# Another order for every engine of a scheduled attention-and-FFT kernel, and waits written latest first

## The chip, the cores and the metric

The kernel runs on one core of a Trainium2 chip. The metric is device time in microseconds (us) of one launch. Before the change three runs gave 243.01, 243.37 and 244.91 us; the median is 243.37. PE is TensorE's matmul stream, PEld its weight loads, DVE VectorE, ACT ScalarE, POOL GpSimd, and SP the SyncE queue, which issues nearly all DMAs.

## The reference

Two branches read the same x (2048 x 640, bf16) and are mixed by a gate per token.

```
g = sigmoid((x * gate_w).sum(-1))
# A: 32 heads of 20, four segments of 512 tokens
for s in range(4):
    p = softmax(q[s] @ k[s].T * scale + causal_mask);  a_dot = p @ v[s]
    a_mem = (phi(q[s]) @ M) / (phi(q[s]) @ z + 1e-6)      # phi(t) = t+1 if t>0 else exp(t)
    o = sigmoid(beta) * a_mem + (1 - sigmoid(beta)) * a_dot
    M += phi(k[s]).T @ v[s];  z += phi(k[s]).sum(0)
a = concat(o) @ wo
# B: a filter in the frequency domain
b = irfft2(rfft2(x) * (w_r + 1j * w_i))
return g * a + (1 - g) * b
```

## The kernel before

The kernel is a list of some 2,300 recorded operations. Each names the engines that may run it with a fixed and a per-element cost, what it reads and writes, and the PSUM banks that it holds. The tuple `ORDER` lists all operations in sequence; a number is twice the operation's index, plus one if it takes the second of its engines. So `ORDER` sets both the order on every engine and who does what. `Sched.schedule` walks the per-engine queues with a cost model, and from the modelled times it chooses PSUM banks (two pools of four, `qk` for scores and `gen` for everything else) and DMA semaphores. `Sched.emit` then writes the instructions, each with the waits that its producers on other engines and its predecessors in a bank or buffer require. Engines run their queues strictly in order.

By segment the operations are as follows.

- `project`: q and k by `proj` (five matmuls of 512 columns, contraction over xT; `projd` for the first two head groups), copied out by `ev_proj` (on ACT, line 523, or DVE, line 525), stored to DRAM (`st_qk`) and loaded back padded to head strips (`pad`, `pad2`). `phi_exp`, `phi_max` and `phi_min` make phi; phi(k) is transposed by DMA (`pkT`, tile `pkn`). `vproj` gives V, which DVE scales (`ev_v`, line 1115).
- `attend`: per pair of head groups five score units (`qk`), their exponentials on ACT (line 1263), causal masks on POOL (line 1284), and the product with V: `pvf` in segments 0 to 2, `pv` in segment 3. In segments 0 to 2 the unnormalised result is copied (`ev_pv`) and stored (`st_u`, tensor u_scr).
- `denominators` of segments 0 to 2: `ld_den` brings the row sums from u_scr, DVE inverts them (`den_rec`, line 1211) and applies the gate (`den_gate`, line 1213, tile `rc`), `st_r` stores `rc` to r_scr.
- `mem_read` (`memrd`) and `mem_update` (`mupd`, from `pkn` and V): the compressive memory.
- `fft`: folds of x on DVE or POOL (lines 901, 906), `F1`, `D`, `T`, the multiplication by the weights (line 1439), `Tb`, `Db` with the G sums (line 1485). Their copies are `ev_F1`, `ev_D`, `ev_Tb`, `ev_Db`.
- `finish_tile` for four token tiles of each segment: `ld_r` brings r_scr back as tile `r`, `ld_u` brings u_scr as `oU`, five `normal` multiply the two (line 1526), the memory part comes by a transposing DMA (`oT`, tile `mT`) and is added (`addmem`, line 1534), and `Fb` plus five `oproj` (lines 514 and 512) accumulate B and A in one bank; `final` copies it out and `st_out` stores it. Segment 3 goes on the chip (`oT3`, `ev_oT3`) with its own copy of wo (`ld_wo2`, 800 KB), and its tiles are stored by `st_part`.

Matmuls use three tile shapes (full array, 20-row strips of `qk`, 32-column strips); a change of shape has a cost in the model (`COST`). The launch begins with ten matmuls on zeros. In `emit` the waits of one operation were written in the order of how much each implies:

```
for key, (val, vc) in sorted(waits.items(), key=lambda q: -len(q[1][1])):
```

Of the kernel before, what the change touches and what calls it, by code (L numbers as in the profile page):

```python
# [12 lines left out]
P = 128  # L13
# [36 lines left out]
class Sched:  # L50
    HOP = 70.0
# [57 lines left out]
    COST = {(0, 1): 94.0, (0, 2): 94.0, (1, 0): 110.0, (1, 2): 110.0, (2, 0): 110.0, (2, 1): 94.0}  # L109

    def schedule(self, pools, order, nsem=56):
# [31 lines left out]
        port = mode = 0  # L143
        level = {k: {q: 0.0 for q in v} for k, v in pools.items()}
# [23 lines left out]
        def head(e):  # L168
# [4 lines left out]
            for p in o.preds:  # L173
                if p.t1 is None:
                    return None
                if p.eng != "pe" or e != "pe":
                    t = max(t, p.t1 + self.HOP)
# [9 lines left out]
            if o.dma:  # L187
                gate = window()
                if gate is not None:
                    t = max(t, gate.t1 + self.HOP)  # L190
            if e == "dve" and o.lock:
                t = max(t, free["pool"])
            elif e == "pool":
                t = max(t, port)
            return t

        while len(self.order) < len(order):
# [21 lines left out]
            if e == "dve" and o.lock:  # L219
                port = t + occ  # L220
            if o.dma:
# [4 lines left out]
                o.t1 = max(ring[:o.width])  # L226
# [11 lines left out]
            o.t1 += lat  # L238
            self.order.append(o)
            for b in o.banks:  # L240
                b.left -= 1
                if b.left == 0:
                    for q in range(b.bank, b.bank + b.n):
                        users[q] = list(b.ops)
                        level[b.pool][q] = max(p.t1 for p in b.ops) + self.HOP
# [3 lines left out]
    def emit(self, *last):  # L249
# [14 lines left out]
        for o in self.order:  # L264
# [3 lines left out]
            for p in o.preds + o.dyn:  # L268
# [5 lines left out]
                if waits.get(key, (0, None))[0] < val:  # L274
                    waits[key] = (val, vc)
            for key, (val, vc) in sorted(waits.items(), key=lambda q: -len(q[1][1])):
                if k.get(key, 0) >= val:
                    continue
                sem = dsem[key] if isinstance(key, int) else prog[key]
                self.eng[e].wait_ge(sem, val)  # L280
                for kk, vv in vc.items():
                    if k.get(kk, 0) < vv:
                        k[kk] = vv
                k[key] = val
            h = o.alts[e][0](self.eng[e])
# [176 lines left out]
class Kern:  # L462
# [34 lines left out]

    def mms(self, items, r, w, prio, name="", extra=0.0, mode=0):

        cost = sum(c * PECOL + 0.75 if mode > 0 else max(c * PECOL + 2.8, 25.4) for _, c in items) + extra  # L500
# [15 lines left out]
        op = self.Sc.op({"pe": (f, cost, 141.0)}, r=r, w=w, prio=prio, name=name, mode=mode)  # L516
        return op

    def copy_alts(self, dst, src, n, engines=("act", "dve"), scale=None):

        alts = {}
        if "act" in engines:
            alts["act"] = (lambda e: e.activation(dst(), src(), ACT.Copy), 65 + 0.833 * n, 110.0)
# [10 lines left out]
    def either(self, fn, n, r, w, prio, name="", after=()):  # L534

        return self.Sc.op({"dve": (fn, 67 + 0.52 * n, 68.0), "pool": (fn, 120 + 1.95 * n, 50.0)}, r=r, w=w, prio=prio, name=name, after=after, lock=True)
# [5 lines left out]
    def dma(self, dst, src, nbytes, r, w, prio, tr=False, name="", after=(), queue="sp"):  # L542
# [14 lines left out]
        "ld_fcat": (400.0, 350.0, 16), "ld_g": (400.0, 1500.0, 16), "ld_gc": (580.0, 200.0, 16), "ld_gw": (420.0, 600.0, 16),  # L557
        "ld_hm": (600.0, 850.0, 16), "ld_r": (570.0, 500.0, 16), "ld_tt": (530.0, 1650.0, 16), "ld_u": (500.0, 450.0, 16),
        "ld_wka": (520.0, 1100.0, 16), "ld_wkb": (450.0, 2200.0, 16), "ld_wqa": (500.0, 1100.0, 16), "ld_wqb": (500.0, 2200.0, 16),
        "ld_wo": (600.0, 700.0, 16), "ld_wo2": (600.0, 3000.0, 16), "ld_wv": (450.0, 3000.0, 16), "ld_x": (450.0, 950.0, 16),  # L560
        "oT": (1300.0, 750.0, 16), "pad2": (370.0, 350.0, 10), "pad": (400.0, 1250.0, 10), ("pkT", 131072): (1260.0, 600.0, 16), ("pkT", 262144): (1280.0, 1100.0, 16),
        ("st_qk", 65536): (450.0, 220.0, 16), ("st_qk", 131072): (480.0, 350.0, 16), ("st_qk", 262144): (480.0, 720.0, 16), "st_g": (430.0, 150.0, 4), "st_o": (660.0, 950.0, 8), "st_out": (560.0, 1900.0, 4),
        "st_part": (430.0, 250.0, 16), "st_r": (480.0, 200.0, 16), "st_u": (520.0, 700.0, 16), ("xT", 131072): (1240.0, 1300.0, 16), ("xT", 262144): (1700.0, 2300.0, 16),
# [16 lines left out]
        46, 0, 90, 26, 74, 23, 2, 4, 36, 24, 6, 8, 28, 10, 12, 72, 14, 16, 30, 18, 20, 178, 64, 34, 202, 66, 68, 44, 42, 70, 93, 214, 52, 190, 48, 94,  # L580
        204, 97, 216, 180, 192, 218, 104, 98, 182, 76, 206, 101, 194, 38, 208, 220, 196, 103, 198, 222, 201, 184, 224, 186, 210, 188, 296, 50, 212,
        256, 298, 362, 78, 300, 536, 32, 80, 274, 538, 258, 83, 302, 260, 262, 276, 130, 278, 264, 84, 54, 280, 106, 266, 282, 1904, 86, 304, 364,
        284, 88, 366, 108, 380, 306, 576, 132, 826, 268, 290, 828, 814, 110, 368, 578, 831, 816, 113, 382, 384, 386, 819, 370, 540, 388, 832, 270,
        834, 410, 412, 272, 836, 414, 416, 391, 418, 552, 372, 490, 420, 288, 492, 494, 114, 496, 498, 554, 118, 820, 822, 134, 336, 500, 240, 137,
        338, 242, 340, 120, 348, 58, 824, 342, 116, 350, 308, 122, 312, 544, 142, 226, 932, 546, 124, 344, 292, 244, 56, 228, 144, 246, 286, 248, 347,
        139, 352, 230, 294, 232, 126, 250, 354, 146, 234, 374, 1906, 149, 237, 1908, 356, 254, 1910, 359, 2094, 151, 238, 1912, 844, 1914, 252, 2124,
        140, 2126, 1916, 2128, 128, 2130, 360, 166, 2096, 40, 846, 2098, 154, 2132, 848, 2100, 2134, 1924, 326, 1926, 314, 2102, 168, 392, 1928, 2104,
        1930, 156, 892, 310, 1932, 152, 838, 1944, 1934, 170, 334, 1946, 158, 894, 840, 324, 316, 1948, 842, 808, 897, 161, 328, 810, 1950, 1952, 394,
        320, 813, 880, 886, 163, 882, 322, 1954, 888, 560, 332, 502, 884, 504, 396, 506, 330, 172, 508, 890, 448, 376, 510, 1936, 398, 450, 436, 512,
        438, 378, 402, 452, 514, 562, 440, 174, 442, 2162, 400, 1962, 2164, 176, 444, 2166, 516, 556, 454, 456, 2168, 446, 165, 2170, 458, 464, 460,  # L590
        466, 406, 1918, 468, 462, 470, 570, 472, 408, 2172, 910, 912, 542, 474, 898, 900, 318, 914, 602, 903, 2150, 548, 604, 2152, 2154, 2156, 2158,
        1920, 2178, 572, 404, 2160, 1966, 2180, 1958, 2182, 1922, 1968, 574, 904, 60, 2184, 2174, 2186, 906, 594, 2188, 1956, 564, 908, 1970, 2176,
        580, 934, 874, 596, 876, 1972, 879, 476, 566, 1974, 62, 478, 480, 550, 1977, 868, 870, 930, 422, 568, 482, 424, 873, 484, 426, 928, 916, 558,
        486, 428, 430, 488, 918, 2136, 432, 598, 2138, 920, 2140, 434, 2142, 856, 582, 858, 1960, 2144, 922, 519, 861, 924, 606, 584, 2146, 936, 1938,
        520, 2148, 926, 588, 523, 1020, 525, 608, 586, 652, 591, 2596, 802, 654, 862, 850, 804, 864, 852, 1940, 2216, 867, 2204, 2206, 2218, 2208,
        2220, 1942, 2210, 2222, 1980, 854, 2224, 2212, 656, 634, 2226, 2214, 1978, 778, 658, 2006, 2228, 636, 780, 2230, 2008, 1982, 2190, 2010, 782,
        2012, 526, 946, 2014, 786, 784, 2192, 948, 1964, 938, 940, 942, 2194, 788, 950, 2196, 945, 2198, 952, 600, 660, 2017, 2200, 790, 662, 2202,
        792, 2018, 976, 978, 1984, 794, 2020, 958, 798, 796, 1986, 960, 980, 954, 2233, 800, 1988, 982, 610, 956, 664, 2038, 612, 1990, 528, 2236,
        2234, 1992, 965, 530, 984, 986, 2040, 1995, 534, 2076, 988, 2078, 962, 2042, 1996, 2000, 1998, 2044, 991, 614, 618, 1016, 2080, 2024, 620,
        2002, 996, 1014, 2082, 2238, 638, 998, 2084, 972, 2004, 2022, 2046, 622, 668, 974, 992, 624, 2086, 2049, 2056, 626, 1018, 994, 1070, 1072,  # L600
        2058, 1074, 666, 2060, 1022, 1076, 642, 1002, 2050, 806, 1104, 1024, 1026, 670, 645, 1001, 2062, 532, 1028, 2270, 2064, 1031, 628, 2036, 2636,
        2252, 2240, 1106, 2272, 630, 2638, 2274, 2254, 640, 2066, 2276, 2106, 676, 616, 2640, 2256, 678, 592, 2258, 1010, 1004, 2243, 2026, 966, 968,
        2052, 2070, 2028, 1013, 632, 692, 971, 1006, 694, 680, 2244, 2642, 1009, 2644, 686, 1032, 2068, 1034, 682, 2246, 646, 1100, 2054, 2090, 1036,
        2030, 2088, 684, 2288, 649, 710, 2034, 2646, 672, 2290, 1039, 2566, 712, 674, 2292, 2598, 2294, 2600, 2306, 2072, 2602, 2110, 2604, 2308,
        2606, 2074, 2568, 2310, 700, 2092, 2108, 2312, 714, 2608, 726, 2112, 2786, 703, 716, 728, 2114, 1044, 2788, 2570, 688, 1062, 1064, 1046, 2790,
# [1001 lines left out]
```

## Time and profile before

| | before |
|---|---|
| median of 3 runs | 243.37 us |
| span of the profiled execution | 245.4 us |
| mean granted TensorE clock | 0.986 |
| instructions | 10243 |
| DVE, ACT, POOL busy | 195.6, 199.9, 166.4 us |
| DMA moved | 42.17 MB |

One execution was profiled; its own time is known only as its span, which is 2.0 us above the median and 0.5 us above the slowest of the three runs. A busy share is an average over stages. PE's busy time includes modelled ends of pipelined matmuls, so a gap of PEld (the weight loads, which run ahead) often shows a wait better than a gap of PE.

### The profile page before, as it was taken

Reading aid. Unit: us, or ns where it says so; the run is one execution under the profiler, and the core shown is the slowest. Engines: PE = TensorE matmul, PEld = TensorE weight load, DVE = VectorE, ACT = ScalarE, POOL = GpSimd, SP = SyncE. Lnnn points to the kernel's source line nnn. Section 1 sums busy time; section 2 is a strip of 40 time slices with the busy share of each in tenths; the row PEclk is TensorE's granted clock in tenths of the full one; section 3 lists DMA queues with packets and bytes.
Section 4 is the critical chain, followed back from the end, with each engine's and each line's share of the span. In section 5 each row is a group of like instructions: output and inputs, shape, how many; then the busy total and the mean of one; then the engine's idle time right before and its main releaser. Section 6 shows DMA issues by size and latency. Waiting matters only on the chain.

```text
span 245.4 us, 10243 instructions
## 1 busy us (share of the span) xinstructions
PE 228.8 (93%) x4347; PEld 140.8 (57%) x4361; DVE 195.6 (80%) x481; ACT 199.9 (81%) x241; POOL 166.4 (68%) x297
## 2 busy tenths in 40 slices
PE   7899999999999999999899999899999997699994
PEld 2574567765455665545556555465454565366794
DVE  0479998889999987989999898989889867435563
ACT  2289698988999999999899889999999976388740
POOL 8513268557969846768947998859898694359730
PEclk9999999999999999999999999999999999589999
DMA  7999959975799875575698661375758997812123
GB/s 168 278 365 208 239 160 178 318 140 164 210 200 174 168 226 143 125 199 135 202 233 234 185 186 53 99 210 146 222 151 194 230 140 96 127 36 85 57 84 108
DMA packets 58928, 42.17 MB, mean 172 GB/s; under 512 B 30020, under 2 KB 55172, under 8 KB 58884
## 3 DMA queue, kind: packets, MB, share of 16 engines
q1 hardware_dynamic: 57844, 40.96, 69.2%
q8 instruction: 34, 0.56, 1.0%
q10 hardware_dynamic: 1040, 0.57, 0.8%
q14 instruction: 10, 0.08, 0.1%
HBM read 23.32 MB, written 12.30 MB: 145 GB/s over the span
## 4 chain that ended last, share of the span: by engine, by line
PE 54%; DVE 18%; ACT 12%; DMA 10%; issue 3%; SPq 1%; DVEq 0%
PE psum L514 48%; ACT ex L1263 9%; PE psum L512 6%; DMA pkn<-phk 4%; DMA r_scr<-rc 3%; DMA xT<-in_A_x_dram 2%; DVE xsb L906 2%; DVE Pt L1439 2%; DVE xf L901 1%; DVE phk L1085 1%; ACT et L1072 1%; DVE oU L1526 1%; DVE G L1485 1%; DVE ub L525 1%; DVE va L1115 1%
## 5 line engine op out<-in xcount | busy, mean ns | idle before, releaser
L1263 ACT ACTIVATE ex<-psum 128x2048 bf16<-128x2048 f32 (+4 forms) x92 | 138.7, 1507 | 16.3 <-PE psum L514 14.3
L1284 POOL TENSOR_SCALAR_AFFINE_SELECT ex<-ex 128x256 bf16<-128x256 bf16 (+2 forms) x224 | 122.1, 567 | 42.0 <-ACT ex L1263 38.4
L514 PE MATMUL psum<-qkp 20*64 20x64 bf16 (+5 forms) x1280 | 32.7, 271 | 4.8 <-issue 2.3
L514 PE MATMUL psum<-xT,wk 128*128 128x256 bf16 (+1 forms) x280 | 34.0, 273 | 0.9 <-DMA wk<-in_A_wk_dram 0.6
L514 PE MATMUL psum<-wv,xT 128*32 128x321 bf16 (+3 forms) x400 | 30.0, 301 | 0.6 <-DVE va L1115 0.3
L514 PE MATMUL psum<-xT,wq 128*128 128x512 bf16 (+1 forms) x121 | 27.0, 380 | 1.3 <-DMA xT<-in_A_x_dram 0.7
L1439 DVE TENSOR_TENSOR Pt<-psum,Wt 128x642 bf16<-128x642 f32 x32 | 25.5, 820 | 2.3 <-PE psum L514 1.9
L514 PEld LDWEIGHTS psum<-qkp 20*64 20x64 bf16 x1280 | 13.4, 103 | 19.5 <-ACT ex L1263 13.2
L514 PEld LDWEIGHTS psum<-xT,wk 128*128 128x128 bf16 (+1 forms) x280 | 19.9, 97 | 7.0 <-DMA wk<-in_A_wk_dram 1.1
L512 PE MATMUL psum<-wo,oU 128*32 128x320 bf16 x480 | 23.4, 313 | 0.5 <-DVE oU L1534 0.5
L906 POOL TENSOR_TENSOR xsb<-xf 128x320 bf16<-128x320 bf16 (+2 forms) x12 | 9.2, 763 | 17.1 <-DVE xsb L906 13.2
L525 DVE CAST ot<-psum 128x320 bf16<-128x320 f32 x21 | 10.1, 491 | 12.9 <-PE psum L512 10.5
L514 PEld LDWEIGHTS psum<-wv,xT 128*32 128x32 bf16 (+1 forms) x400 | 14.3, 96 | 8.3 <-issue 2.4
L514 PE MATMUL psum<-big,Ac 128*128 128x160 bf16 (+2 forms) x96 | 18.1, 258 | 0.7 <-DVE Pt L1439 0.3
L1115 DVE TENSOR_TENSOR va<-psum,ebx 128x320 bf16<-128x320 f32 x32 | 15.2, 483 | 4.2 <-ACT gate L1113 2.1
L514 PE MATMUL psum<-big,Cp 128*128 128x321 bf16 (+1 forms) x96 | 18.0, 302 | 0.2 <-DVE G L1485 0.2
L514 PE MATMUL psum<-ex,va 128*32 128x64 bf16 (+3 forms) x576 | 17.4, 256 | 0.7 <-DVE dn L1152 0.3
L1485 DVE TENSOR_TENSOR G<-eo,psum 128x320 bf16<-128x320 f32 x32 | 14.7, 482 | 3.9 <-PE psum L514 2.8
L512 PEld LDWEIGHTS psum<-wo,oU 128*32 128x32 bf16 x480 | 12.4, 100 | 8.8 <-issue 4.2
L514 PE MATMUL psum<-tt,Yt 128*128 128x256 bf16 (+1 forms) x96 | 16.5, 275 | 0.3
L514 PEld LDWEIGHTS psum<-ex,va 128*32 128x32 bf16 x576 | 11.1, 96 | 9.7 <-POOL ex L1284 3.4
L1072 ACT ACTIVATE et<-qu 128x512 bf16<-128x512 bf16 x25 | 15.6, 630 | 0.2
(99 smaller groups left out, 391.9 us busy)
## 6 DMA issues: line engine op xcount, KB each, us to landing
qkp<-qk_scr SPq DMA_DIRECT2D x28, 160.0 KB
tt<-tab_tt SPq DMA_DIRECT2D x8, 512.0 KB, 4.3
qk_scr<-qu SPq DMA_DIRECT2D x12, 256.0 KB, 3.1
u_scr<-ub SPq DMA_DIRECT2D x12, 256.0 KB, 3.9
xsb<-in_A_x_dram SPq DMA_DIRECT2D x8, 320.0 KB, 6.8
oU<-u_scr SPq DMA_DIRECT2D x15, 128.0 KB, 2.9
out_dram<-ot SPq DMA_DIRECT2D x12, 160.0 KB
Wt<-in_B_w_r_dram SPq DMA_DIRECT2D x16, 80.2 KB, 2.6
```

The lines of the kernel that those rows point to most:

```text
L512: h = e.matmul(dst, wt, r_, start=st, stop=sp_, **{**kw, "tile_position": (0, q), "skip_group_check": True})
L514: h = e.matmul(o_, l_, r_, start=st, stop=sp_, **kw)
L525: alts["dve"] = (lambda e: e.tensor_copy(dst(), src()), 67 + 1.04 * n, 68.0)
L901: self.either(lambda e, r=r, op=op: e.tensor_tensor(xf.ap(r * 642, [321, 2], [1, 320]), xs.ap(o, [D, 2], [1, 320]), xs.ap(o + 320, [D, 2], ...
L906: self.either(lambda e, dst=dst, src=src, d0=d0, n=n, op=op: e.tensor_tensor(xs.ap(o + dst, [D, 2], [1, n]), xf.ap(src + d0, [321, 2], [1, ...
L1072: self.one("act", lambda e: e.activation(et.ap(0, [1, L]), qsl(), ACT.Exp), L, [qb], [b("et", pi_)], late, name="phi_exp")
L1085: fmin = lambda e: e.tensor_tensor(dst(), dst(), et.ap(0, [1, L]), ALU.min)
L1115: self.one("dve", lambda e: e.tensor_tensor(va.ap(i * H * VW + h0 * VW, [VW, nh], [1, DH]), self.ps(bank, 0, [DH, nh], [1, DH]), self.ebx. ...
L1263: self.one("act", lambda e, d=d, q=q: e.activation(self.ex.ap(*d), self.ps(bank, *q), ACT.Exp, scale=SC), n, [bank], [self.exb(s, 2 * pr + ...
L1284: self.one("pool", lambda e: e.affine_select(self.ex.ap(e0 + d0, [1280, 4], [1, n], np_=np_), self.ex.ap(e0 + s0, [1280, 4], [1, n], np_=np_),
L1439: self.one("dve", lambda e, ri=ri, Pt=Pt, Wt=Wt, wo_=wo_, bank=bank: e.tensor_tensor(Pt.ap(ri * 322, [644, 2], [1, KD]), self.ps(bank, 0, ...
L1485: self.one("dve", lambda e, q=q, n2=n2, bank=bank, eo=eo: e.tensor_tensor(self.G.ap(n2 * D + 639 * q, [1 - 2 * q, 320]), eo.ap(q, [1, 320] ...
```

## The change

No operation is added or taken away. Four things differ.

1. `ORDER` is another sequence. On PE 210 of the 1072 adjacent pairs of operations are kept, on DVE 45 of 480, on ACT 77 of 248, on POOL 55 of 292, on SP 17 of 231. The middle displacement is 5 operations or so on PE, 11 on DVE, 6 on ACT, 4 on POOL, 3 on SP. 14 more operations run on DVE, 11 fewer on ACT's queue (12 fewer copies, and the load of `wk` that was on SP), 2 fewer on POOL, 1 fewer on SP.
2. The model's constants are changed, which moves bank choices and DMA semaphores, since these follow the modelled times: a delay per pair of engines in place of one delay, landing of a DMA 500 ns later, DVE and POOL overlapping at the shared port by some ns, costs of a few operations.
3. The waits of one operation are written in the order of the modelled time at which they end, latest first.
4. The `m_mask` products on POOL (line 1361) are marked `lock` for the model.

The start of the orders, and the two stretches that the prediction speaks of:

```
SP before:  ld_x1 xT0 ld_beta ld_wka xT1 xT2 ld_wkb ld_x0 ld_fcat ld_x4 ld_x2 ld_wv ...
SP after:   xT0 xT1 xT2 ld_x1 ld_wkb ld_x0 ld_beta ld_x2 ld_wv ld_x3 ld_fcat ld_x4 ...
ACT before: ld_wqa exp(beta) ev_projd ...
ACT after:  ld_wqa ld_wka ev_projd ev_projd exp exp(beta) ...

SP before:  ld_den oT ld_u ld_wo2 st_g pad oT ld_u ld_u ld_u ld_u ld_u st_r st_out pad oT ld_r st_out st_out oT oT ld_g st_out oT oT
SP after:   ld_den ld_u ld_u pad ld_u ld_u ld_u ld_u st_r pad oT ld_r st_out ld_wo2 oT ld_g st_out st_out oT st_out oT st_out oT

DVE before: den_rec normal G G den_gate normal pv_den pv_rec normal pv_mul addmem addmem G ev_Db G final final G
            pv_den G pv_rec pv_mul final [5 normal] pv_den pv_rec pv_mul addmem ...
DVE after:  den_rec G normal normal normal den_gate G addmem G addmem G G pv_den pv_rec pv_mul ev_Db G G
            [5 normal] final pv_den pv_rec pv_mul addmem G G pv_den G pv_rec G pv_mul addmem ...
```

The diff, cut to its core:

```diff
 class Sched:
-    HOP = 70.0
+    HOPS = {
+        "pe": {"pe": 0.0, "act": 52.0, "dve": 55.0, "pool": 60.0, "sp": 60.0, "dma": 50.0},
...
+    FREE, PORT, LATE = 52.0, (85.0, 55.0), 500.0
...
-                    t = max(t, p.t1 + self.HOP)
+                    t = max(t, p.t1 + self.HOPS[e]["dma" if p.dma else p.eng])
...
-                o.t1 = max(ring[:o.width])
+                o.t1 = max(ring[:o.width]) + self.LATE
...
-            for key, (val, vc) in sorted(waits.items(), key=lambda q: -len(q[1][1])):
+            kept = []
+            for key, (val, vc, t1) in sorted(waits.items(), key=lambda q: -len(q[1][1])):
                 if k.get(key, 0) >= val:
                     continue
-                sem = dsem[key] if isinstance(key, int) else prog[key]
-                self.eng[e].wait_ge(sem, val)
+                kept.append((t1, dsem[key] if isinstance(key, int) else prog[key], val))
...
+            for t1, sem, val in sorted(kept, key=lambda q: -q[0]):
+                self.eng[e].wait_ge(sem, val)
...
     ORDER = (
-        46, 0, 90, 26, 74, 23, 2, 4, 36, 24, 6, 8, 28, 10, 12, 72, 14, 16, 30, 18, 20, 178, 64, 34, 202, 66, 68, 44, 42, 70, 93, 214, 52, 190, 48, 94,
...
+        4626, 4628, 4542, 4540, 4647, 4630, 4584, 4556, 4633, 4546, 4544, 4600, 4568, 4570, 4572, 4654, 4648, 4602, 4558, 4604, 4574, 4652, 4606,
```

## The prediction

> **What bounds the kernel now.** I read the page first: busy shares, the 40 slices, the chain. Then one table of stretches, the chain of waits in order of time, and the timeline of the SP queue late in the span.
>
> ```profile
> span 245.4 us, 10243 instructions
> ...
> PE 228.8 (93%) x4347; PEld 140.8 (57%) x4361; DVE 195.6 (80%) x481; ACT 199.9 (81%) x241; POOL 166.4 (68%) x297
> ...
> PE   7899999999999999999899999899999997699994
> ...
> PEclk9999999999999999999999999999999999589999
> ...
> PE 54%; DVE 18%; ACT 12%; DMA 10%; issue 3%; SPq 1%; DVEq 0%
> ```
>
> TensorE (PE) bounds it: 93% busy, and it carries over half of the chain. Its two bad slices (7 and 6) lie near 205 us, and right there the granted clock falls to 0.5 and 0.8. The stretches say how much is idle where (columns: stretch, its length, busy us and instructions of PE, PEld, DVE, ACT, POOL, granted clock, DMA share, GB/s):
>
> ```profile
> 0.00:12.00 12.00, 9.24 (x134) 4.65 (x135) 3.29 (x7) 2.64 (x5) 8.82 (x13) 1.00 0.89 220
> 24.00:204.00 180.00, 172.85 (x3081) 103.33 (x3093) 160.40 (x396) 164.64 (x197) 133.73 (x246) 1.00 0.74 181
> 204.00:216.00 12.00, 8.71 (x197) 5.16 (x200) 7.07 (x18) 5.68 (x9) 4.29 (x6) 0.73 0.80 105
> 216.00:240.00 24.00, 24.00 (x732) 18.19 (x728) 12.47 (x31) 16.14 (x20) 16.04 (x27) 0.99 0.22 66
> ```
>
> PE idles 2.76 us in the first 12 us, 7.15 us in the 180 us of the middle, 3.29 us in 204 to 216. In that last stretch some 4.8 us of work (211.4 to 216.2) also ran at clock 0.50. The chain of waits, in order of time (start, length, what), names the causes at both ends:
>
> ```profile
> 3.61 4.16 DMA xT<-in_A_x_dram
> ...
> 193.49 0.31 DVE rc L1213
> ...
> 194.85 6.89 DMA r_scr<-rc
> 201.74 0.02 issue
> 201.76 2.35 DMA r<-r_scr
> ...
> 209.06 2.35 issue
> ```
>
> At the start, PE works on the second transposed piece of x, issued only at 3.61. Late, the softmax denominators of segment 2 go out (`st_r`, from `rc`) and come back (`ld_r`): from the end of `rc` (193.80) to the first product with it (204.13) 10.3 us pass. The row "issue" is a stall of PE with no release behind it; one packet of PE's instruction queue was under way (208 to 210: one packet, 1.2 us). The timeline of the SP queue (start, length of the issue) shows what stood ahead of `st_r`:
>
> ```profile
> 187.79 0.60 SPq L548 DMA_DIRECT2D wo<-in_A_wo_dram  x1
> ...
> 189.25 2.33 SPq L546 DMA_TRANSPOSE mT<-o_scr  x1
> 191.63 3.17 SPq L548 DMA_DIRECT2D oU<-u_scr  x5
> 194.85 0.60 SPq L548 DMA_DIRECT2D r_scr<-rc  x1
> ```
>
> **The change part by part.** The matmuls are the same 4361, and in the two orders the changes between the three tile shapes number 229 and 230. At a change the weight load idles 0.20 to 0.27 us in the timeline, so this costs at most 0.3: nothing.
>
> *Who copies.* Twelve PSUM copies move from ACT to DVE on balance (six of `ev_D`, six of `ev_Tb`, three `ev_oT3`, one each of `ev_proj` and `ev_projd`, less one `ev_pv` and four `final`), and DVE gains four folds and a `normal`, and loses a gate table and two adds. By the rows (ACT 0.54, 0.60, 0.59; DVE 0.52, 0.68, 0.69; `final` 0.44 and 0.49) ACT loses about 7 us and DVE gains about 9: ACT 193, DVE 204 of 245. Neither passes PE's 229, so I cost it at nothing. The cover is DVE's remaining fifth; gone for one copy, it costs 0.7.
>
> *Start.* On SP the second and third transposes stood behind an `xsb` load (0.40), the first transpose (1.22), `beta` (0.57) and `wk` (0.42); now they stand behind the first transpose alone, and `wk` goes out on ACT's queue. The second can be issued at about 0.79+1.22 = 2.0 in place of 3.61: 1.6 us sooner. If the DMA engines (share 0.89 over 12 us) were the limit, nothing is won. I take 1.2, nearer the queue's end, because the `xsb` load that shared the engines now comes behind. `beta` moves later by some 4 us; its first user, the V copy at 20.3, hides it.
>
> *Waits.* The built program keeps the wait that is written first on the instruction itself and puts the others into a semaphore instruction ahead of it. PE has 80 instructions with two or more waits (now 81). In the trace such a semaphore instruction takes 51 ns on PE and the next weight load begins typically 25 ns later. With the latest first, 76 ns go wherever the other order stood and PE really waited: between 0 and 80 x 0.076 = 6.1. PE waits for POOL 13 times, the kind with a partner wait; half of those: 0.5.
>
> *Middle.* Of PE's adjacent pairs only 210 of 1072 stay, but attention keeps its place (counted by PE work done, most scores move under 1 us); fillers are permuted. The memory update of segment 1 moves 1 to 6 us later, behind its transposed load `pkn` (1.4 us of PE and PEld waits). What the rest does no row shows: not more gain than half of the idle 7.15, and as much loss if fresh waits of the present size (42 waits for ACT, 0.3 each) appear in a quarter more places. I take 1.0, from -3.5 to +3.5, near the `pkn` row.
>
> *End.* Before `st_r` SP issued, after `ld_den` (185.27): two transposes (1.29, 2.33), six `ld_u`, the 800 KB load of `wo2`, and two small ones, 9.6 us in all; `st_r` left 1.05 us after `rc` into engines with a share of 1.19 (192 to 198), and took 6.89. Now only six `ld_u` and one `pad` stand between, 4.4 us with gaps, while `rc` needs about 3.8 (landing of u_scr loads, median) + 3.4 (DVE work up to `rc`) = 7.2 after `ld_den`. SP then waits for `rc`, and the backlog has 2.8 us to drain. Landing: 1.8 (40 KB stores) to 6.9; I take 3.0, near the small stores, for `st_r` is 32 KB. With `ld_r` at 2.6 the 10.3 us become 5.7. In DVE's new order 5.2 us of work fill that time, then come the five `normal`, then `final`, `pv_den`, `pv_mul`, the G sums. So DVE idles 0.5, where before it idled 1.41, and PE's 0.5 us wait for the add at 208.09 goes. The stall of 2.35 and the half clock's cost (4.8 us of work at 0.5: 2.4) I count half: a fetch that comes late under DMA load can come late again, but with no wait ahead of it the hole is shorter. End: 0.5 + 2.4 = 2.9, between -5.5 and +8.
>
> The row: 0.9 us of PEld waiting, then 2.6, and the clock was 0.50 for the next windows. The Trainium skill (TensorE: Matmul & The Clock Gate, Part 1) says that the clock halves after an idle window of about 3.4 us; the trace agrees in size, with 3.3 us of waits nearly back to back. By that rule a hole of 2.35 alone would keep the clock and the end would give 4.1 instead.
>
> Sum: 1.2 + 0.5 + 1.0 + 2.9 = 5.6; the profiled span would be 239.8. The span lies 2.0 above the median (243.37) and 0.5 above the slowest run (244.91). If the timed runs hold the late hole, they go to 243.37 - 5.6 = 237.8; if none does, to 243.37 - 2.7 = 240.7. Their spread of 1.9 settles neither; I take the middle, 239.2.
>
> **The rivals.**
> *Only the start comes.* The middle gives nothing and the late hole stays or was never in the timed runs: 243.37 - 1.2 - 0.5 = 241.7, and up to 245 if the middle loses. For it: PE is 96% busy in the middle, and every fine interlock there is new; also if waits in another order change nothing. Against: the SP rows.
>
> *The denominators come late and now block DVE.* On the other side. The five `normal` stood behind `final`, `pv_mul` and two G sums, and now stand ahead of them. Those free the four general PSUM banks. If `st_r` again takes 6.9, the wait is 6.9 + 2.8 = 9.7 against 5.2 of work: DVE stops for 4.5 us, PE runs out of banks about 1 us later, idles 3.5, and the clock halves for 6.8 us (3.4 lost). Also `wo2` is now issued right behind `ld_r`, ahead of two mT transposes: 800 KB at about 200 GB/s are 4 us for a load that lands in 3.8 to 7.2. Price: 3.5 + 3.4 + 4 = 10.9, less the 5.3 of the old hole, less 1.7 of start and waits: +3.9 on a run with the old hole and more on one without: about 248. It decides when `r` lands over 3 us later than DVE's cover.
>
> *The middle closes too.* Half of its idle time goes (3.5 in place of 1.0), and the whole late hole: 235.5. For it: PE has no other bound above 204 us of DVE.
>
> **How the numbers follow.** Forecast 0.44, only the start 0.27, late denominators 0.17, middle too 0.12. One per cent (2.43 us) is about what a measurement tells from no change. Faster (under 240.94): nearly all of the forecast's cases and of the last: 0.54. Same: the start alone, and a little of the forecast: 0.29. Slower (over 245.8): 0.17. The range 235 to 246 takes in the first two cases and half of the last, and leaves out about 0.06 below and 0.14 above. The forecast's own range is 237 to 241.
>
> **What would show it.** Start right: the second transpose issued near 2.0 and PE's first dense stretch about a microsecond earlier. End right: `r_scr` lands in under 4 us, DVE's wait for `r` is under 1 us, no 0.5 in the clock row past slice 30. Waits right: fewer short PEld waits on semaphores of two engines. Wrong: DVE waiting 3 us or more for `r`, PE behind it on a bank, or a new half-clock stretch in the middle; or the idle time of 24 to 204 above 10 us.

## The result, and the profile after

| | before | changed |
|---|---|---|
| median, run side by side (4 runs each) | 244.14 us | 246.18 us |
| profiled execution: span | 245.4 us | 243.8 us |
| its granted clock | 0.986 | 0.990 |

The changed kernel is slower: 1.0142 times the time of before, 95% interval 1.0108 to 1.0175. A second measurement gave 1.0213 (1.0155 to 1.0271). The ratios here leave out slow executions, those over 1.5% above the fastest of the same kernel, while the medians in us take in all. The forecast was 239.2 us in a range of 235 to 246; both the sign and, by 0.2 us, the range were missed. Note that the span went *down* while the time went up: the profiled execution of before was an unusually long one (e1, below), so the two spans say nothing of which kernel is faster.

The page after: span; busy times; PE by slices; granted clock by slices; shares of the chain.

```profile
span 243.8 us, 10266 instructions
...
PE 229.3 (94%) x4361; PEld 139.5 (57%) x4361; DVE 201.8 (83%) x495; ACT 195.8 (80%) x229; POOL 167.3 (69%) x295
...
PE   7989999999799999999998989999989997999994
...
PEclk9999999999999999999999999999999999799998
...
PE 60%; DVE 19%; DMA 6%; ACT 5%; issue 4%; SPq 4%; DVEq 0%
```

The late hole was not closed: PE has a 7 in the slice of 201 to 207 us, and the clock has one in the next. ACT and DVE came out at 195.8 and 201.8 (193 and 204 were said). The stretches, with the columns of before:

```profile
0.00:12.00 12.00, 10.53 (x149) 5.12 (x150) 2.19 (x5) 2.84 (x4) 6.59 (x10) 1.00 0.84 220
24.00:204.00 180.00, 172.82 (x3081) 101.41 (x3078) 167.49 (x414) 160.78 (x187) 133.98 (x242) 1.00 0.74 182
204.00:216.00 12.00, 10.67 (x281) 6.93 (x278) 7.32 (x18) 7.79 (x9) 7.13 (x12) 0.86 0.56 87
216.00:240.00 24.00, 24.00 (x740) 18.95 (x732) 12.92 (x33) 14.00 (x18) 15.07 (x27) 1.00 0.33 76
```

The first 12 us hold 1.3 us more of PE's work, the middle idles as much as before (7.18 us), and at 204 to 216 the clock is 0.86. The chain in order of time (start, length, what):

```profile
2.08 1.29 SPq L561
...
7.10 6.82 DMA xsb<-in_A_x_dram
13.94 0.50 DVE xf L916
...
14.68 1.30 DVE ebx L895
...
205.33 1.33 issue
```

The second transpose goes out at 2.08, as forecast, but the chain of the start is now another one: a load of `xsb` (x for the folds), then DVE's folds and `ebx` (what DVE computes from `beta`). Late, neither `r_scr` nor `r` is on the chain, and "issue" is. SyncE's queue there (start, length):

```profile
193.26 0.36 SPq L563 DMA_DIRECT2D r_scr<-rc  x1
...
194.21 1.78 SPq L561 DMA_TRANSPOSE mT<-o_scr  x1
196.04 0.59 SPq L563 DMA_DIRECT2D r<-r_scr  x1
196.73 0.64 SPq L563 DMA_DIRECT2D out_dram<-ot  x1
197.41 0.48 SPq L563 DMA_DIRECT2D wo<-in_A_wo_dram  x1
```

`rc` ends at 193.23 and the first of the five `normal` starts at 199.05: 5.8 us, against 5.7 forecast and 10.3 before. The load of `wo2` (800 KB) goes out at 197.41; before, at 187.79.

### The profile page after: what moved, and what is told of

It is laid out like the page before. It is cut to its first block, busy times and chain, and to the rows that moved or that the text cites. A ratio compares the mean times of both kernels' runs of the same rounds, so it can differ in the third digit from the quotient of the medians.

```text
span 243.8 us, 10266 instructions
## 1 busy us (share of the span) xinstructions
PE 229.3 (94%) x4361; PEld 139.5 (57%) x4361; DVE 201.8 (83%) x495; ACT 195.8 (80%) x229; POOL 167.3 (69%) x295
## 4 chain that ended last, share of the span: by engine, by line
PE 60%; DVE 19%; DMA 6%; ACT 5%; issue 4%; SPq 4%; DVEq 0%
PE psum L529 53%; PE psum L527 7%; ACT ex L1278 4%; DMA xsb<-in_A_x_dram 3%; DMA pkn<-phk 3%; DVE G L1501 3%; SPq L563 2%; DVE Pt L1455 2%; SPq L561 2%; DVE Bt L540 1%; DVE Yt L1460 1%; DVE mem L1172 1%; DVE qu L540 1%; DVE Cp L540 1%; DVE mem L1175 1%
## 5 line engine op out<-in xcount | busy, mean ns | idle before, releaser
L529 PE MATMUL psum<-xT,wk 128*128 128x256 bf16 (+1 forms) x280 | 32.9, 275 | 0.8 <-DVE q L540 0.7
L529 PE MATMUL psum<-xT,wq 128*128 128x512 bf16 (+1 forms) x135 | 31.1, 387 | 0.5 <-DVE Ac L540 0.4
L527 PE MATMUL psum<-wo,oU 128*32 128x320 bf16 x480 | 22.6, 309 | 0.0
L529 PE MATMUL psum<-big,Cp 128*128 128x321 bf16 (+1 forms) x96 | 18.5, 303 | 1.5 <-DVE mem L1175 0.5
L529 PE MATMUL psum<-big,Ac 128*128 128x321 bf16 (+2 forms) x96 | 17.7, 257 | 0.0
L540 DVE CAST ot<-psum 128x320 bf16<-128x320 f32 x17 | 8.1, 489 | 9.8 <-PE psum L527 8.0
L540 DVE CAST Bt<-psum 128x322 bf16<-128x322 f32 x26 | 13.5, 518 | 2.2 <-PE psum L529 2.1
```

Source lines behind the costliest of these rows:

```text
L527: h = e.matmul(dst, wt, r_, start=st, stop=sp_, **{**kw, "tile_position": (0, q), "skip_group_check": True})
L529: h = e.matmul(o_, l_, r_, start=st, stop=sp_, **kw)
L540: alts["dve"] = (lambda e: e.tensor_copy(dst(), src()), 67 + 1.04 * n, 68.0)
```

## The experiments

There were eighteen runs, each beside the kernel before on the same chip; e1 and e16 are the two kernels once more. Two readings are used throughout. One is the ratio. The other follows each TensorE operation through two traces and takes the mean of its delay by stretch, so that a loss can be placed. All delays here are against one reference, e4 below (the old order built by the new code). It is the shortest execution profiled, 241.3 us where the median of e4 is 242.6, and each run has one trace, so small delays prove little.

**Which part of the change?** e1 is the kernel before, unchanged. e2 and e3 exchange the order of waits alone:

```diff
 e2 = before            e3 = changed
-sorted by -len(vc)    -latest first
+latest first          +sorted by -len(vc)
```

> The kernel before once more, for a second profile of it, since the first one's span (245.4 us) is long against its timed runs. For the changed kernel a run is 1.9 us longer than its span, so the timed runs of before (243.0 to 243.4) should have spans of about 241.2. If the late hole (PE stalled 2.35 us near 209, clock 0.50 for some 7 us) was peculiar to that one execution, this profile has a span near 241.3, no 0.5 in the clock row, and the hole is no part of what the change could win. If the hole is in every execution, the span is 245 again.

Measured: 243.43 us, span 241.7, clock 1.000. The late hole with 0.5 in the clock row isn't in this execution. Over all 101 executions of the kernel before that were run beside e1 to e18 the granted clock was 0.997 or more in 66 (median 242.5 us), 0.992 or 0.993 in 27, and as low as in the profiled one (0.986 or less) in 8.

> The order and the model of before; only the waits of one operation are written latest first. Theory ORDER (the new sequence itself costs the 1.4 per cent): 0.995 to 1.001 of before. Theory WAITS (the latest wait on the instruction itself is dearer, for instance because it stands behind the semaphore instruction): 1.01 or more. My prediction counted a gain of 0.5 us for it: 0.998.

Measured: 242.36 us, ratio 0.9963 (0.9920 to 1.0006).

> The changed kernel with the waits in the way of before. ORDER: 1.012 to 1.018, as the change. WAITS: 1.000 to 1.004.

Measured: 249.18 us, 1.0193 (1.0104 to 1.0283). The new wait rule may gain 0.4%, which the interval does not separate from nothing; it loses 0.1% at most.

```diff
 e4 = changed, with the old sequence
-ORDER = (46, 0, 90, 26, ...)
+ORDER = the tuple of before
```

> The changed kernel with the order of before: the new model (which chooses PSUM banks and DMA semaphores) and the new writing of waits, without the new sequence. ORDER: 0.995 to 1.003. A third theory, MODEL (the loss comes from other banks and semaphores, which add waits between an operation and the former user of its bank): 1.01 or more.

Measured: 242.58 us, 0.9975 (0.9931 to 1.0019), span 239.6, clock 0.999. So the model's constants (banks, semaphores) cost 0.2% at most beside the old sequence, and the loss comes with the new one.

**Which stretch?** Each kernel takes one order for all that the old order begins up to a cut, and the other order for the rest.

```diff
 ORDER
 e5: new up to  24 us, then old
 e6: new up to 188 us, then old
 e7: old up to 188 us, then new
 e8: new up to 110 us, then old
```

> The new order for everything that the old order begins in its first 24 us, the old order for all the rest; the new waits. Against the old order in the new wait rule (ratio 0.9975 to before). Theory END (the loss is made at 192 to 208 us, the start's lead of 2 to 3 us at 13 to 16 us is eaten by 23 us): 0.9975, within 0.003. Theory START (the earlier transposes upset the later loads and cost time from then on): above 1.003. If the lead is kept by the old order's next stretch, as the prediction had it: 0.9925 (1.2 us better).

Measured: 243.94, 1.0041 (1.0004 to 1.0078).

> The new order up to 188 us, the old order from there. Theory END: the new order stood 0.9 us behind at 188 us, so 0.9975 + 0.9/243 = 1.001; faster than the changed kernel by 3 us or more. Theory SPREAD (the loss is made all along, the plan of the new order being no better in any stretch): 1.010 or more.

Measured: 246.60, 1.0176 (1.0109 to 1.0242).

> The old order up to 188 us, the new order from there: the mirror of the run before. Theory END: 3 to 4 us lost, so about 1.011. Theory SPREAD: below 1.004.

Measured: 246.03, 1.0154 (1.0117 to 1.0192).

> The new order up to 110 us, where it stood about 1 us ahead of the old one by the units of TensorE, the old order from there. Theory END with a lead that lasts: 0.9935, faster than both kernels. If the lead at 110 us is only a shift of which work is done first: 0.9975. Theory START or SPREAD: 1.003 or more.

Measured: 243.69, 1.0051 (1.0018 to 1.0085). Mean delay in us of TensorE's operations against e4, by the time at which e4 begins them (e1, e13 and e15 for comparison; a figure moves by up to 0.3 with the width of the stretch):

```
from us   e1   chg   e5    e8    e6    e7    e13   e15
   12    0.0  -0.9  -1.1  -0.6  -1.1  -0.1  -0.7  -1.1
   24   -0.2   0.4   1.1   0.2   1.0  -0.5   0.4   0.3
  104    1.3   0.8   1.4  -0.1   1.3   0.6   0.8   0.3
  170    1.3   1.1   0.9   0.5   1.5   0.0   1.0   0.5
  192    1.8   2.2   0.9   0.5   3.4   2.2   3.6   1.7
  208    2.4   4.8   2.4   0.9   3.4   4.8   5.0   2.0
  228    2.2   4.0   2.5   0.9   3.4   3.9   4.0   1.2
```

Three things are read off it. The new start leads by 0.6 to 1.1 us at 12 and has lost it by 24. Up to 110 us the new order keeps pace (e8). From 170 on it loses about 3 us. The column e1 is the measure for this: the kernel before, at whole clock, ends 2.2 us behind e4 as well. And the column of the changed kernel is its best trace: e16 and e3, the other two with this order on every engine, are 2.8 and 1.7 us behind at 104 already, 4.4 and 4.1 at 192, and 7.2 and 9.3 at 228. So one trace doesn't fix how the loss is spread. But e6 and e7 each lose nearly all of it, so the pieces don't add: a cut makes a seam, where each order expects the other to have done something already (e6 lost 1.9 us between 170 and 192, before and at its seam). Neither END nor SPREAD holds as stated. The windows of the start show where the lead goes; first e4, then the changed kernel (its first 12 us stand above):

```profile
0.00:12.00 12.00, 9.98 (x132) 4.53 (x133) 3.35 (x7) 2.46 (x4) 8.81 (x13) 1.00 0.88 217
12.00:24.00 12.00, 11.75 (x156) 7.76 (x156) 10.00 (x25) 10.79 (x15) 3.80 (x5) 1.00 1.14 288
```

```profile
12.00:24.00 12.00, 10.96 (x132) 7.08 (x138) 11.10 (x28) 10.06 (x14) 4.57 (x6) 1.00 1.08 279
```

In the first 12 us DVE did 3.35 us of work in the old order and does 2.19 in the new one. Its rows say which work is missing; first e4, then two of the changed kernel (L895 is the first step of `ebx`):

```profile
6.10 1.05 DVE L895 TENSOR_SCALAR ebx<-ebx 128x32 f32<-128x32 f32 x1 [4.85 <-ACT ebx L893]
```

```profile
9.96 0.69 DVE L540 CAST qkp<-psum 128x512 bf16<-128x512 f32 x1 [8.71 <-PE psum L529]
...
14.59 1.38 DVE L895 TENSOR_SCALAR ebx<-ebx 128x32 f32<-128x32 f32 x1
```

The old order does `ebx` and the first fold (at 7.68) while DVE has nothing else. In the new one a copy of PE's first product comes first, so DVE stands until 9.96; the first fold follows at 10.83, a later one waits 0.73 us for its load, and `ebx` falls into 12 to 24, where DVE is busiest (11.10 of 12). There PE, which had gained 0.55, loses 0.79.

**Loads, or VectorE?** By now the trace of the changed kernel showed TensorE waiting, at 186 to 198 us, for VectorE only (who is waited for: total, times, longest), where e4 has no row at all:

```profile
PE psum L529 <- DVE G L1501: 0.6, 2, 0.4
PE psum L529 <- DVE gT L1023: 0.3, 1, 0.3
PE psum L529 <- DVE on L1340: 0.2, 1, 0.2
```

```diff
 e9:  changed, but SP's queue in the old order
 e10: e4, but SP's queue in the new order
```

> The changed kernel with SyncE's queue (all loads and stores) in the old order, the other four engines in the new one. Theory COMPUTE (the loss comes from the order of VectorE, ScalarE, GpSimd and TensorE): about as slow as the changed kernel, 1.012 or more of the kernel before. Theory DMA (the loss comes from when loads and stores go out: the fold loads behind the transposes, wo2 behind ld_r): at most 1.003.

Measured: 290.7 us, 1.1972.

> The mirror: the old order on the four computing engines, SyncE's queue in the new order. Theory COMPUTE: 0.9975 to 1.004 (the start may lose about 1 us, as the fold loads come later than the old VectorE order wants them). Theory DMA: 1.012 or more.

Measured: 279.58 us (the fastest of four 275.29). (The load of `wk` goes with the exchange: on SyncE in e9, on ACT in e10.) Both theories are missed by far: either SyncE queue costs 32 to 48 us beside the other order's computation. What waits at the head of the queue holds up all behind it: in e9 SyncE stood 28.4 us, in nine pieces of up to 7.2, for TensorE alone. An order is one piece over all engines; swapping one engine's queue measures the mismatch, not the queue.

```diff
 e11: changed, DVE's queue at 184 to 197 us
-G20 G21 normal G gate G ... normal normal normal den_gate G26 addmem8 G27 addmem10 G24 G25 pv
+G20 G21 gate G G normal ... normal G26 G27 normal normal den_gate G24 G25 pv addmem8 addmem10
```

> The changed kernel with eight VectorE operations moved by a few places at 184 to 197 us: a gate copy and two G sums before a normal, two G sums before two normals, and the two adds addmem 8 and 10 behind two G sums and pv_mul 0. Theory VECTOR (non-urgent products and adds stand before the sums that free the PSUM banks; TensorE waits 0.7 + 0.5 + 0.6 + 0.6 us for them): 1.6 to 2.0 us less, and where the clock then stays whole another 1.7: ratio to before 1.000 to 1.008, with granted clocks of 0.997 and more in part of the runs. Rival FETCH (the hole that costs the clock is TensorE's late instruction fetch at 205 us, whatever VectorE does): at most 1 us less, 1.010 to 1.015, and clocks of 0.993 and below in all runs.

Measured: 248.83 us, 1.0214 (1.0160 to 1.0267), clock 0.986 or less in all six. Neither theory's range holds. Against the changed kernel, TensorE's delay fell by 0.7 us up to 196 to 200, as wished, and rose by 3.1 up to 204 to 208. The chain of e11 says what came in its place:

```profile
200.25 5.53 DMA out_dram<-ot
205.80 0.45 ACT ot L538
```

SyncE's transpose into `mT` waits until `addmem 8` has read the old one. With that add 4.2 us later (197.78 for 193.55), the store of the output behind it in SyncE's queue left at 200.25 in place of 196.73 (1.3 us of this lateness was there at 190 already), and ACT's next `final` waited for its buffer. An add that looked idle was holding a queue. This is read off one trace; the adds were not moved alone.

```diff
 e12: e4, start of SP's queue (ld_wka moves to ACT)
-ld_x1 xT0 ld_beta ld_wka xT1 xT2 ...
+ld_x1 xT0 xT1 xT2 ld_beta ...
```

> The old order with one step of the new start alone: the load of wk goes out on ScalarE's queue and beta behind the third transpose, so that the second transpose goes out near 2.5 us instead of 3.6; the fold load stays first. Theory START-KEPT (the gain of the start is lost only because the fold load was put back): 0.9925 to 0.995, faster than both kernels. Rival: the gain is eaten whatever the loads do, as VectorE's folds and the later loads set the pace up to 24 us: 0.996 to 0.999, as the old order in the new wait rule.

Measured: 243.16 us, 0.9989 (0.9953 to 1.0024): nothing is gained, as the rival said. But its trace has no lead that could have been kept: the second transpose goes out at 2.53, and PE's first product with x still begins at 6.6, against 5.7 in e4 and 5.5 in the changed kernel. So it doesn't show what eats the lead of the new order.

**The late instruction fetch.** The 1.33 us of "issue" at 205.33 lie inside one row of matmuls, so no semaphore is waited for. Rows of PE at that place, and the packet of PE's instruction queue between 203.5 and 206 (the trace puts its start at 204.25):

```profile
204.80 0.53 PE L529 MATMUL psum<-va,ex 128*128 128x21 bf16 x15
206.66 0.47 PE L529 MATMUL psum<-va,ex 128*128 128x21 bf16 x13 [1.33 <-issue]
```

```profile
q8 instruction: 1, 0.02, 2.8%
```

PE's 4,456 weight loads and waits come in 34 such packets, 131 apiece. Counted from one fetch to the next, 240 lie ahead of this one, so it starts nearly a whole block late; by the mean it was due near 200 us, when 800 KB of `wo2` were moving (330 to 360 GB/s from 199.6 to 202.5). The Trainium skill (Runtime: NRT & Kernel Launch, Instruction fetch mechanics) says that the next 16 KiB block is fetched while the current one runs and that this is mostly hidden; in this trace 1.33 us of it are not.

```diff
 e13: changed, SP's queue        e14: e4, SP's queue
+ld_wo2                         -ld_wo2
 ld_u14 ld_u10 ... st_r          st_g ... st_r ... ld_r
 ... ld_r st_out                +ld_wo2
-ld_wo2                          st_out
```

> The changed kernel with one load moved: the 800 KB load of wo2 goes out in front of the loads ld_u 14, 10, 13, 12 and of st_r (near 189 us) in place of behind ld_r (197.4 us). Theory FETCH (in the changed kernel the block of TensorE's instructions that is due near 200 us is fetched only at 204.25, behind this load's transfer; TensorE runs dry for 1.33 us and the clock is halved for 3.41): the fetches come 90 to 180 instructions apart again, no wait of over 1 us near 205 us, clocks of 0.997 and more in most runs, and 1.3 + 1.7 = 3.0 us less than the changed kernel: ratio to before 1.000 to 1.005. Theory ORDER (the loss is in the waits for VectorE, and the clock falls because of these): no change, 1.012 to 1.017, clocks of 0.993 and below.

Measured: 245.49 us, 1.0095 (1.0052 to 1.0138). In its trace the fetches from 190 us on are 98 to 160 apart and no wait near 205 passes 0.5 us. The clock was 0.998 or more in 5 of 12 executions; in both measurements of the changed kernel together, in 1 of 8. The time lies between the two theories. Beside e16, the changed kernel run with it on the same chip (1.0155 to 1.0271), the gain is clear of the noise; beside the first measurement (1.0108 to 1.0175) it isn't. In the one trace, though, e13 ends as far behind e4 as the changed kernel: it lost as much before 204 us, by waits for VectorE and a halved clock at 198.2.

> The mirror, in the old order under the new wait rule (0.9975, clock 0.997 and more in 7 of 10 runs): the load of wo2 goes out behind ld_r (near 198 us) in place of 187.5 us. Theory FETCH: the fetch due near 200 or 204 us comes late, TensorE stands 1 to 2.5 us, and the clock falls in most runs: 1.008 to 1.015. Theory ORDER: 0.995 to 1.001, clocks as before (the loads of u, st_r and ld_r go out 0.6 us earlier).

Measured: 243.13 us, 1.0010 (0.9975 to 1.0045), clock whole in 8 of 12. No late fetch: one went out at 200.4, just ahead of the transfer (`wo2` issued at 198.55), the next at 204.8. The mirror failed: moving the load late isn't enough by itself. That it does harm only where a fetch falls due inside the transfer fits e14 and every other trace with the late load. In the changed kernel, e3 and e16 the 131st weight load or wait since the last fetch falls at 200.4, 202.2 and 202.6, as the transfer begins or runs; the fetch comes some 2 us after its end, and PE stands. In e11 a fetch got out at 201.5, ahead of the transfer, and in e18 (below) the next is due at 206.1, behind it: no such stall in either. No run moved a due fetch in or out of the transfer by itself, so the rule is argued, not shown.

```diff
 e15: e13, DVE's queue: e11's moves without addmem8 and addmem10
```

> The run with wo2 early, and in addition six VectorE operations moved by a few places at 184 to 194 us: a gate copy and two G sums before one normal, two G sums before two normals; the adds addmem 8 and 10 stay where they are, for SyncE's oT 3 and what is queued behind it waits for them. Theory VECTOR: 0.7 to 1.2 us less than the run with wo2 early alone (its TensorE waits of 0.7 and 0.5 us go). Rival: another wait comes last, no difference within 0.5 us.

Measured: 243.78 us, 1.0033 (1.0002 to 1.0063), clock 0.997 or more in 10 of 12. The median is 1.7 us below e13's, but not for the reason given. Among executions at whole clock the two are equal (medians 243.70 for e15, 243.78 for e13, 1.2 us above the kernel before), and the waits moved rather than went. Windows of e4, of the changed kernel and of e15:

```profile
184.00:198.00 14.00, 13.91 (x298) 7.58 (x301) 12.81 (x30) 12.54 (x16) 10.88 (x20) 1.00 0.87 220
...
204.00:212.00 8.00, 7.43 (x230) 4.85 (x218) 6.34 (x16) 6.45 (x8) 4.80 (x8) 1.00 0.89 121
```

```profile
184.00:198.00 14.00, 12.89 (x247) 6.60 (x244) 12.23 (x30) 12.01 (x16) 11.12 (x18) 1.00 0.63 173
...
204.00:212.00 8.00, 6.67 (x173) 4.49 (x173) 4.95 (x13) 4.21 (x5) 5.86 (x9) 0.79 0.52 104
```

```profile
184.00:198.00 14.00, 12.62 (x247) 6.37 (x249) 12.79 (x29) 11.74 (x16) 10.91 (x20) 1.00 0.76 211
...
204.00:212.00 8.00, 8.00 (x251) 5.89 (x252) 6.05 (x15) 6.80 (x8) 6.21 (x9) 1.00 0.31 59
```

At 204 to 212 e15 is whole again (8.00 at clock 1.00). At 184 to 198 it still lacks 1.3 us of PE against e4, with DVE as busy in both (12.79 and 12.81). So it isn't the amount of VectorE's work; that the new order does other things first is the likely reason.

> The changed kernel once more, beside the others on the same chip: 1.0142 again, within 0.004. Theory FETCH: the late fetch near 204 us, the wait behind it and the half clock are there again in its profile; if they were chance, they are not.

Measured: 248.02 us, 1.0213 (1.0155 to 1.0271). The late fetch recurs: 243 weight loads and waits after the one before, start at 207.42, and 1.65 us of "issue" before the matmul at 210.00. e3, which has this order and this SyncE queue too, shows the same (240 apart, start at 206.8, 1.51 us). But the half clock that was expected behind it isn't there: the profiled execution of e16 kept its clock whole to 246.8 us and still took 248.66 us. So a halved clock is not needed for the changed kernel to be slow.

**The start inside the new order.**

```diff
 ORDER up to 24 us
-new
+old          (e17: in e15; e18: in the changed kernel)
```

> The run with wo2 early and the G sums first (1.0033), and in addition the old order for what the old order begins in its first 24 us. Theory THREE PARTS (what the new order loses is its start, the late instruction fetch and the places of a few VectorE operations, each measured alone, the start at 0.0066 of the time by the run that had only the new start): 1.0033 - 0.0066 = 0.997, as fast as the old order in the new wait rule, within 0.003. Rival MORE (other places of the new order cost as well, and the start's price depends on what follows): 1.002 or more.

Measured: 244.65 us, 1.0080 (1.0042 to 1.0118).

> The changed kernel with the old order for the first 24 us and nothing else. Theory THREE PARTS: 0.0066 below the changed kernel (1.0142 and 1.0213 in its two measurements): 1.0075 to 1.0147, with the late fetch near 204 us still there. Rival: the start matters only to the order that follows it in the run with the new start alone: 1.014 or more.

Measured: 247.38 us, 1.0185 (1.0136 to 1.0234). THREE PARTS falls: putting the old start back makes neither e15 nor the changed kernel faster (1.0080 for 1.0033, with intervals that overlap, and 1.0185 for 1.0142 and 1.0213). The new start doesn't explain the loss. The late fetch that was expected in e18 is not there (178 apart, and no "issue" of over 0.2 us behind 186 us). It is as slow without it: PE waits 0.69 and 1.27 us for G sums at 187 and 197, and the clock is halved from 198.9 to 205.7. e7 is a second such case, with `wo2` early, no late fetch and 1.0154.

Over the kernels that follow the new order from 24 us to the end, the clock was whole in 3 of 24 executions with `wo2` late (changed, e3, e11, e16, e18) and in 25 of 36 with it early (e13, e15, e17). At whole clock those 3 took 247.1 to 249.4 us and those 25 took 242.4 to 246.4, in the middle 243.8. So the place of this load matters beyond the clock, and the stall at the fetch cannot be all of it. No kernel of the study beats the one before by more than the measurement is uncertain; e2 and e4 come nearest.

## Why the prediction was wrong, by its own steps

*Start, 1.2 us.* The mechanism and nearly the size were right as far as PE's first stretch: transpose at 2.08, lead of 0.9 us at 12 to 16. It failed at "`beta` moves later by some 4 us; its first user, the V copy at 20.3, hides it". The first user on DVE is `ebx`, which moved from 6.10, where DVE stood idle, to 14.59, among folds and copies. The `xsb` loads behind the transposes were counted as relief for the DMA engines and not as a delay for the folds, one of which waits 0.73 us. By 24 us nothing was left. How much either takes is open.

*Waits, 0.5.* e2 gives 0.9 us at the middle of an interval that reaches from 2 us to nothing. Not refuted, not shown.

*Middle, 1.0 of gain.* Against e4 the changed kernel loses 0.7 us between 24 and 170 (0.4 to 1.1), within the bounds of 3.5 either way. The sign is not shown: e1, in the old order, loses 1.5 there (-0.2 to 1.3). The idle time of 7.18 equals the old 7.15, so the sum should have had nothing here.

*End, 2.9.* This is the step that failed. Its r chain was right (5.8 us for 5.7) and worth nothing. The 2.4 of it came from a late hole that was an accident of the profiled execution: e1 doesn't have it, 66 of 101 executions keep the whole clock, and 8 fall as low. The spread of the three runs, which "settles neither", was the place to stop: the gain should have been counted at the share of executions that have the hole, a third at most. And "a fetch that comes late under DMA load can come late again, but with no wait ahead of it the hole is shorter" was the right suspicion with the wrong conclusion: the new order has a late fetch in three of its traces, with 1.33 to 1.65 us of stall, and the change itself put the 800 KB of `wo2` where the fetch falls due. With the load back in front (e13) the late fetch is gone, and the ratio is 1.0095 for 1.0142 and 1.0213: 1.1 to 2.9 us, clear of the noise against the second alone. That the stall carries all of this is not shown (e18 has the late load, no stall, and 1.0185).

*Who copies, at nothing.* "Neither passes PE's 229" looked at the whole span. At 184 to 198 us PE waits 1.1 us in all for DVE operations that read PSUM, and has 1.0 us less work than in e4 (12.89 for 13.91). But DVE is no busier there than in e4 (12.23 and 12.81), where PE doesn't wait for it. So the amount of copies was rightly counted at nothing; DVE's order at this place had no price in the sum. Which DVE operations stand wrongly is not settled: e11 and e15 moved the suspects, and other waits came last.

*The rival "denominators late".* It had the slower sign, the place and one link of the mechanism: G sums, which free PSUM banks, now stand behind `normal`. What holds `normal` up in the changed kernel is not `r` but the load of `oU`: DVE stands 0.35 us for it at 191.67, in e16 0.43, in e18 0.78, in e7 2.51, and in before, e1 and e4 not at all from 184 us on. No run tried that load earlier. For `r` DVE stood 1.41 us in before and not at all in the changed kernel; only e7 (2.76) and e11 (1.69) come near what the rival describes. Of the rival's pieces, `wo2` behind `ld_r` cost time (e13), in three traces through PE's instructions; a user of `wo2` that came late was not seen.

Two sums don't come out as they are meant. "If none does, to 243.37 - 2.7" drops the 0.5 of DVE's idle time with the hole; with it the time is 240.2. And 235.5 for "the middle closes too" counts the whole late hole in half of the runs; counted in all it gives 232.9. Neither changes the sign.

Together, in the two profiled executions: the changed kernel is 1.5 us behind e4 at 188, 2.4 at 200, 4.8 at 208 and 4.0 at 228. Between 188 and 200 lie 0.6 of waits for VectorE; between 200 and 208 the stall of 1.33 and a halved window (1.7 at the most), less a wait of 0.5 at 206 that e4 alone has. The 1.5 before are not taken apart, and e1 shows that the old order can lose as much. Without the late hole the sum still promised 3.2 us. The sign turned because start and middle gave nothing that lasted, and because the fetch and the waits for VectorE had no price in it.

## What to carry to other kernels

Before a hole in one profile is counted as a gain, look at whether the other executions have it: a second profile or the clock of each execution tells. When a step is moved forward on an in-order queue, price what is put behind it, by its readers' engines. And look at where large loads fall against the fetches of the busiest engine's own instructions: in three traces here the fetch came late and the engine stood.

## What the runs showed of the hardware

The clock can halve after holes far shorter than 3.4 us. In windows of 3.41 us on the grid of the clock's own changes, the changed kernel:

```profile
204.80:208.21 3.41, 2.08 (x73) 1.65 (x71) 2.33 (x7) 1.60 (x3) 3.14 (x5) 1.00 0.84 146
208.21:211.62 3.41, 3.41 (x85) 2.03 (x85) 1.82 (x6) 1.55 (x2) 1.54 (x4) 0.50 0.12 27
```

A hole of 1.33 us (PE busy 2.08 of 3.41) was followed by exactly one window at 0.50. The prediction had drawn from the Trainium skill (TensorE: Matmul & The Clock Gate, Part 1) that it takes an idle window of about 3.4 us; no such window is here. Nor is one in the trace of before, which the prediction took to agree. There the clock fell at 209.42, 0.36 us into the stall of 2.35, so most of the stall came after it:

```profile
206.01:209.42 3.41, 2.22 (x79) 1.35 (x76) 3.27 (x10) 1.97 (x3) 1.80 (x2) 1.00 0.34 80
209.42:212.83 3.41, 1.42 (x21) 0.79 (x24) 0.64 (x2) 1.15 (x2) 0.90 (x3) 0.50 0.85 136
```

And e16, whose hole of 1.65 us (208.35 to 210.00) lies across the border of two windows, kept its clock:

```profile
205.85:209.27 3.42, 2.40 (x47) 1.70 (x48) 2.41 (x7) 2.51 (x3) 2.58 (x4) 1.00 0.59 171
209.27:212.68 3.41, 2.68 (x90) 2.17 (x93) 2.09 (x8) 1.59 (x2) 1.80 (x2) 1.00 1.02 101
```

Busy time alone is no threshold either. e6 kept its clock behind the first row, e5 lost it behind the second:

```profile
189.92:193.33 3.41, 2.17 (x44) 0.90 (x47) 2.67 (x6) 2.15 (x3) 3.09 (x5) 1.00 0.94 277
```

```profile
204.18:207.59 3.41, 2.84 (x88) 2.10 (x89) 3.31 (x10) 2.72 (x4) 2.14 (x2) 1.00 1.00 111
```

What the gate counts stays open. One halved window, with whatever waits go with it, costs 1.4 us here: 243.9 against 242.5 us, the medians of executions of the kernel before with a clock of 0.992 or 0.993 and with a whole one.
